# Attention step with its transposes in one group, and the last columns' transpose in the free columns of the next scores' bank

## The chip, the cores and the metric

The kernel runs on one core of a Trainium2 chip. The metric is the device time of one execution in microseconds (us). Three runs of the kernel before gave 1032.47, 1027.31 and 1030.96 us, so the median is 1030.96 us.

## What is computed

The reference is an attention layer followed by two feed-forward layers. The change touches only the attention.

```
scores = (q @ k.T) / sqrt(64) + bias(h, i, j)        # B=4, H=8, S=576, D=64; bias from a small MLP on positions
attn   = softmax(scores, axis=-1)                    # over 576 columns
x      = attn @ v                                    # -> 2304 tokens x 512
x      = leaky_relu(x @ w_in, 0.01) @ w_out          # d_ff = 2048
out    = per token: one of 8 experts (largest cosine), gate * (relu(x @ w1[e]) @ w2[e])
```

## The kernel before, in words

The work has three phases. Phase 1 (`phase1`, L563) holds the position bias, the attention and the first matmul of the first feed-forward layer (`up_units`, L513, tile `psh`). Phase 2 is the second matmul and the routing, phase 3 the experts. The trace puts the attention of phase 1 between 33 and 515 us.

The attention runs over 80 steps (L572). A step is a batch entry b, a half hf of the rows, a pair p of heads and a block ib of 128 rows. Half 0 has the blocks 0 and 1, half 1 the blocks 2, 3 and 4, and the steps of one (b, hf, p) are a group. In a step with ib of 0 to 3 the two heads of the pair are two tiles of 128 rows; the block ib = 4 has 64 rows of each head, which share one tile. There are 64 steps of the first kind and 16 of the second. One step has these parts:

- `scores` (L398): for one head, four matmuls into a two-bank PSUM tile `pss` (pool `psS`, two such tiles): two matmuls into columns 0 to 287 of the first bank (jh = 0), two into columns 0 to 287 of the second (jh = 1). A bank holds 512 columns, so columns 288 to 511 of both stay unused. DVE then adds the bias that lies in the tile `prob` and reduces it to the row maximum (L418).
- `exps` (L423): ACT replaces `prob` by its exponentials (L426).
- `normalise` (L431): `prob` is divided by its row sums: on POOL for b = 0 (L444), and else head 0 on DVE (L442) and head 1 on ACT (L440).
- `transposes` (L456): for one head four 128x128 transposes into one bank `pst` (pool `psT`, two banks), and a copy to `pth`. That copy is on ACT for head 1, and for head 0 on ACT where b = 0 and on DVE else.
- `transpose_tail` (L472): one transpose of the 64 last columns of head 0 and the 64 first of head 1, into a tile `psx` of the same pool `psT`, and a copy to `ptt` (L487), on ACT where b = 0 and on DVE else.
- `values` (L491): at the end of a group, the 20 matmuls `psv` that read `pth` and `ptt`. `values_out` (L647) copies their result out in the first step of the group that follows.

The loop of phase 1 (L660 to L704) writes a step n in this order: transposes of head 0, `values_out`, the tail's transpose, the scores of head 0 of step n + 2, the normalising of step n + 1, side jobs (loads and splits of other operands), filler work worth half a quota, the exponentials of head 0 of step n + 2, the transposes of head 1, the scores of head 1 of step n + 2, side jobs, filler work, its exponentials. The filler is the bias (`psb`, L270) in the first 8 steps and `psh` after that, 12 matmuls at a time.

Each engine's instructions are put in their final order ahead of the run, by a planner that goes by estimated durations: where an instruction's inputs are not ready by its estimate, a later one that is ready goes first. Each engine then runs its list in order on the chip. The DMAs of the loads stand in one list on SP; among them are those that fill `prob` with the bias for a later step (L387 to L392), which wait until the transposes of the step that had the buffer are done.

Of the kernel before, what the change touches and what calls it, by code (L numbers as in the profile page):

```python
# [7 lines left out]
F32 = mybir.dt.float32  # L8
# [109 lines left out]
def new_w_in(p):  # L118
    return [p.tile([128, KD, FF // 2], F32R, name=f"wi{k}") for k in range(2)]


def w_in_split(nc, e, f):

    raw = e.cv.tile([128, KD * 256], U32, tag="w_raw", name="w_raw", bufs=2)
    src = e.w_in.rearrange("(k p) n -> p k n", p=128)
    nc.sync.dma_start(out=raw.rearrange("p (k n) -> p k n", k=KD), in_=src[:, :, 256 * f:256 * f + 256])
    yield
    t = e.cv.tile([128, KD * 128], F32, tag="w_t", name="w_t", bufs=2)
    yield from convert_f64(nc, raw, t)
    yield  # L130
    hi, lo = w_in_columns(e, f)
    t = t.rearrange("p (k n) -> p k n", k=KD)
    COPY[WIN_HI[f // 4]](nc, hi, t)
    LO[WIN_LO[f // 4]](nc, lo, t, hi)
# [153 lines left out]
class Attention:  # L288
# [106 lines left out]

    def scores(self, st, h):  # L398
        nc, e = self.nc, self.e
        b, hf, p, ib = st  # L400
        kt = self.kv[b, p]
        hi, lo = self.qs[b, hf, p]
        tail = self.qtail[0]
        pr, stat = self.prob[st]
        ps = e.psS.tile([128, 2, 512], F32, tag="s", name="pss")
        o = 128 * (ib - HALVES[hf][2][0])
        if ib == 4:
            ops = [(tail[:, 256 * hh + 128 * k:][:, :128], 640 * hh) for hh in range(2) for k in range(2)]
        else:
            ops = [(t[:, h, o:o + 128], 576 * h) for t in (hi, lo)]  # L410
        for jh in range(2):
            for k, (lhsT, c0) in enumerate(ops):
                nc.tensor.matmul(  # L413
                    ps[:, jh, :288], lhsT=lhsT, rhs=kt[:, c0 + 288 * jh:][:, :288],
                    start=(k == 0), stop=(k == len(ops) - 1),
                )
        prv = pr[:, h].rearrange("p (a j) -> p a j", a=2)
        nc.vector.tensor_tensor_reduce(  # L418
            out=prv, in0=ps[:, :, :288], in1=prv,
            scale=-0.125, scalar=3.0e38, op0=ALU.add, op1=ALU.min, accum_out=stat[:, 0, h:h + 1],  # L420
        )
# [47 lines left out]
        else:  # L469
            COPY[PROB_T[h][b]](nc, ph[:, h, :, o:o + 128], ps.rearrange("p (c i) -> p c i", c=4))  # L470

    def transpose_tail(self, st):  # L472

        nc, e = self.nc, self.e
        b, hf, p, ib = st
        pr, _ = self.prob[st]
        pt = self.pt[1]
        o = 128 * (ib - HALVES[hf][2][0])
        ps = e.psT.tile([128, 512], F32, tag="t", name="psx")
        copy = COPY[PROB_T[0][b]]  # L480
        if ib == 4:
            nc.tensor.transpose(ps[0:64, :128], pr[:, 0, 512:576], e.ident)
            for h in range(2):
                copy(nc, pt[64 * h:64 * h + 64, o:o + 64], ps[0:64, 64 * h:64 * h + 64])
            return
        nc.tensor.transpose(ps[:, :128], pr.rearrange("p h j -> p (h j)")[:, 512:640], e.ident)  # L486
        copy(nc, pt[:, o:o + 128], ps[:, :128])  # L487
# [75 lines left out]
def phase1(ctx, tc, e):  # L563

    nc = tc.nc
    early = tc.tile_pool(name="early", bufs=1, side="left")
    e.bout = early.__enter__()
    e.late = None
    at = Attention(nc, e)
    fl = Filler()  # L570
    groups = [(b, hf, p) for b in range(B) for hf in range(2) for p in range(NP)]
    steps = [g + (ib,) for g in groups for ib in HALVES[g[1]][2]]  # L572
    ns = len(steps)
    start = {}
    for n, st in enumerate(steps):
        start.setdefault(st[:3], n)


    todo = {}

    def put(n, pos, f, *args):
        todo.setdefault((max(n, 0), pos), []).append((f, args))

    def side(n, pos):
        for f, args in todo.pop((n, pos), ()):
            f(*args)

    for k, g in enumerate(groups):
        b, hf, p = g
        n0 = start[g]  # L590
        if k >= 2:
            put(n0 - 5, 1, at.q_load, g)
            put(n0 - 4, 1, at.q_hi, g)
            put(n0 - 3, 0, at.q_lo, g)
        if hf == 1:
            put(n0 - 3, 1, at.q_split_tail, g)
        if hf == 0 and k >= 2:
            m = n0 - 4 if b == 0 else start[b - 1, 1, p] + 3
            put(m, 0, at.kv_load, b, p)
            put(m, 1, at.kv_hi, b, p)  # L600
            put(m + 1, 0, at.k_lo, b, p)
            put(m + 3, 1, at.v_load, b, p)

    def spread(n, pos, job, gap):

        k = 2 * n + pos
        put(k // 2, k % 2, lambda: spread_on(k, iter(job()), gap))

    def spread_on(k, it, gap):
        try:  # L610
            next(it)
        except StopIteration:
            return
        put((k + gap) // 2, (k + gap) % 2, spread_on, k + gap, it, gap)

    for f in range(KF):
        spread(2 + f if f < KF // 2 else 3 + f, 0, lambda f=f: w_in_split(nc, e, f), 1)
    for c in range(KF):
        spread(20 + 2 * c, 0, lambda c=c: w_out_narrow(nc, e, c), 1)

    bias_setup(nc, e)
    bu = bias_units(nc, e, WIDE)
    for k in range(32):
        if k == 20:
            for g in groups[:2]:
                at.q_load(g)
                at.q_hi(g)
                at.q_lo(g)
            for p in range(2):
                at.kv_load(0, p)  # L630
                at.kv_hi(0, p)
                at.k_lo(0, p)
                at.v_load(0, p)
        next(bu)
    fl.add(bu)
    for n in range(4):
        at.load_bias(steps[n])
    loaded = 4
    for n in range(2):
        for h in range(2):  # L640
            at.scores(steps[n], h)
            at.exps(steps[n], h)
    at.normalise(steps[0])

    xs = prev = None

    def values_out():  # L647
        nonlocal prev, xs
        if prev is None:
            return  # L650
        pb, ph, pp = prev
        if pp == 0:
            pool = e.xp if ph == 0 else e.late
            xs = [pool.tile([128, KD, HALVES[ph][1]], F32R, tag=f"x{i}{ph}", name=f"x{i}", bufs=1) for i in range(2)]
        at.x_split(prev, *xs)
        if pp == NP - 1:
            fl.add(up_units(nc, e, pb, ph, *xs))
        prev = None

    for n, st in enumerate(steps):  # L660
        g = st[:3]
        b, hf, p = g
        first = start[g] == n
        last = st[3] == HALVES[hf][2][-1]

        quota = 40 * 800.0 / 6.5 if n < 8 else KF * 1600.0 / 8 if hf == 0 else (13 if b == 0 else 17) * 1280.0 / 12
        nx = steps[n + 2] if n + 2 < ns else None
        while loaded < ns and at.free:
            at.load_bias(steps[loaded])
            loaded += 1  # L670
        if first:
            at.new_group()
        at.transposes(st, 0)
        values_out()
        at.transpose_tail(st)
        if nx:
            at.scores(nx, 0)
        if n + 1 < ns:
            at.normalise(steps[n + 1])
        side(n, 0)  # L680
        fl.run(quota / 2)
        if nx:
            at.exps(nx, 0)
        if st[3] != 4:
            at.transposes(st, 1)
        if nx and nx[3] != 4:
            at.scores(nx, 1)
        side(n, 1)
        at.done(st)
        if n == 7:  # L690
            fl.drain()
        else:
            fl.run(quota / 2)
        if nx and nx[3] != 4:
            at.exps(nx, 1)
        if last:
            at.pop_group(g)
            if n == 7:
                early.__exit__(None, None, None)
                e.late = ctx.enter_context(tc.tile_pool(name="late", bufs=1, side="left"))  # L700
                e.wi.append(new_w_in(e.late))
                at.free.append(PROBS)
            at.values(g)
            prev = g  # L704
    at.x_split(prev, *xs)
    fl.add(up_units(nc, e, prev[0], prev[1], *xs))
    return fl


def w_out_narrow(nc, e, c):  # L710

    raw = e.cv.tile([128, 2 * DM], U32, tag="w_raw", name="wo_raw", bufs=2)
    r = slice(128 * c, 128 * c + 128)
    nc.sync.dma_start(out=raw, in_=e.w_out[r])
    yield
    t = e.cv.tile([128, DM], F32, tag="w_t", name="wo_t", bufs=2)
    yield from convert_f64(nc, raw, t)
    nc.sync.dma_start(out=e.wo_d[r], in_=t)
# [738 lines left out]
```

## Time and profile before

| what | us |
|---|---|
| median of three runs | 1030.96 |
| the profiled execution, its own time | 1027.66 |
| its span, first to last instruction | 1025.9 |
| TensorE (PE) busy | 985.7 |
| VectorE (DVE) busy | 682.8 |
| ScalarE (ACT) busy | 547.8 |
| GpSimd (POOL) busy | 103.0 |

The profiled execution is 3.30 us shorter than the median, inside the spread of the three runs. The span leaves 1.8 us of the execution's own time outside. PE stands for the matmuls, PEld for the loads of their stationary operand. The end of a matmul in the trace is modelled, so the distance from one start to the next says more than the length of one.

### The profile page before, as it was taken

The page shows a single profiled execution, that of the slowest core. Times are in us where ns is not written, and L with a number is a line of the kernel's source. Part 1 is how long each engine was busy: PE and PEld are TensorE (multiplying, and loading weights), DVE is VectorE, ACT ScalarE, POOL GpSimd, SP SyncE. Part 2 cuts the span into 40 slices and gives each one's busy share as a digit, 9 for nine tenths or more (in the row PEclk, how much of TensorE's full clock was granted, in tenths as well). Part 3 has the DMA queues.
Part 4 walks back from the last instruction along what each step waited for, and adds up shares of the span by engine and source line. Part 5 has one row for each costly group of instructions (what it writes and reads, how often), then busy time and mean ns, then how long its engine had stood idle before and what let it go on. Part 6 is the DMA issues. An engine that isn't in the chain of part 4 may idle for free.

```text
span 1025.9 us, 19107 instructions
## 1 busy us (share of the span) xinstructions
PE 985.7 (96%) x6294; PEld 809.2 (79%) x6294; DVE 682.8 (67%) x1719; ACT 547.8 (53%) x1102; POOL 103.0 (10%) x112
## 2 busy tenths in 40 slices
PE   5899999999999999999999999999999999999995
PEld 2355788988889898998888888888877888888884
DVE  8888999889865687767675766579892255313312
ACT  5778787556665666556453333344552455324422
POOL 2332431000000000000000000001002111211210
PEclk9999999999999999999999999999998999999998
DMA  7868899989754566546195533338305256313410
GB/s 247 256 202 247 251 297 310 319 284 288 223 172 142 177 205 196 154 129 183 49 294 171 166 111 117 120 103 280 101 11 216 66 203 254 120 49 106 143 42 23
DMA packets 137602, 180.17 MB, mean 176 GB/s; under 512 B 19841, under 2 KB 89857, under 8 KB 137362
## 3 DMA queue, kind: packets, MB, share of 16 engines
q1 hardware_dynamic: 115554, 149.31, 46.9%
q10 hardware_dynamic: 18576, 19.03, 5.3%
q0 software_dynamic: 3360, 10.49, 3.0%
q8 instruction: 52, 0.85, 0.3%
q14 instruction: 60, 0.49, 0.2%
HBM read 196.18 MB, written 43.94 MB: 234 GB/s over the span
## 4 chain that ended last, share of the span: by engine, by line
PE 81%; DVE 7%; DMA 6%; issue 3%; ACT 1%; POOL 1%; SPq 0%; DVEq 0%; ACTq 0%; POOLq 0%
PE psx L784 19%; PE psh L525 15%; PE pu L1272 10%; PE pd L1303 9%; PE pss L413 7%; PE psv L500 7%; PE pst L464 5%; PE psb L270 3%; DMA wo_raw<-in_w_out_dram 3%; DVE mk L224 2%; PE pt L1283 1%; DMA w_t<-wo 1%; PE pt L1255 1%; DMA qraw<-in_q_dram 1%; PE psx L486 1%
## 5 line engine op out<-in xcount | busy, mean ns | idle before, releaser
L525 PE MATMUL psh<-x,wi 128*128 128x256 f32 (+1 forms) x1536 | 226.4, 297 | 1.4 <-DVE hst L532 1.3
L525 PEld LDWEIGHTS psh<-x,wi 128*128 128x128 f32 x1536 | 211.0, 189 | 3.6 <-DVE hst L532 2.9
L426 ACT ACTIVATE prob<-prob,stat 128x576 f32<-128x576 f32 x144 | 111.3, 773 | 66.2 <-DVE stat L418 58.7
L418 DVE CUSTOM_DVE_ANT_0 prob<-pss,prob 128x576 f32<-128x576 f32 x144 | 108.0, 752 | 20.5 <-PE pss L413 16.5
L784 PE MATMUL psx<-woh,gh 128*128 128x512 f32 x288 | 113.1, 393 | 0.3 <-ACT gh L70 0.3
L784 PE MATMUL psx<-wol,gh 128*128 128x512 f32 x288 | 112.7, 391 | 0.0
L784 PE MATMUL psx<-woh,gl 128*128 128x512 f32 x288 | 112.2, 390 | 0.0
L70 ACT ACTIVATE gh<-g 128x512 fp32r<-128x512 f32 x72 | 45.3, 631 | 115.2 <-PE psx L784 99.9
L464 PE MATMUL pst<-ident,prob 128*128 128x128 f32 x576 | 89.4, 278 | 4.4 <-DVE pth L78 2.1
L464 PEld LDWEIGHTS pst<-ident,prob 128*128 128x128 f32 x576 | 65.9, 140 | 23.0 <-issue 13.9
L1241 POOL DMA_INDIRECT xg<-x,gidx x22 | 25.3, 1152 | 577.6 <-DMA ws<-in_mw_dram 549.1
L413 PE MATMUL pss<-kt,qhi 128*128 128x288 f32 x256 | 81.3, 332 | 0.0
L270 PE MATMUL psb<-mk,cf 128*32 128x79 f32 (+49 forms) x640 | 60.8, 420 | 13.9 <-POOL cf L254 6.8
L413 PE MATMUL pss<-kt,qlo 128*128 128x288 f32 x256 | 72.3, 297 | 0.0
L500 PE MATMUL psv<-pth,vs 128*64 128x256 f32 (+1 forms) x512 | 72.1, 413 | 0.0
L1303 PE MATMUL pd<-w2h,hth 128*128 128x512 f32 x160 | 67.8, 424 | 3.9 <-ACTq L1228 3.9
L801 DVE SCALAR_TENSOR_TENSOR junk<-x1s,en 128x512 bf16<-128x512 f32 x96 | 66.1, 689 | 3.1 <-DMA en<-en_d 2.1
L82 DVE TENSOR_TENSOR htl<-pt,hth 128x512 fp32r<-128x512 f32 x40 | 27.1, 689 | 57.8 <-ACT hth L70 57.8
L70 ACT ACTIVATE pth<-pst 128x512 f32<-128x512 f32 (+1 forms) x100 | 54.4, 548 | 20.6 <-PE pst L464 12.8
L1272 PE MATMUL pu<-w1h,xh 128*128 128x512 f32 x160 | 65.1, 407 | 0.3 <-ACT xh L70 0.3
L1303 PE MATMUL pd<-w2h,htl 128*128 128x512 f32 x160 | 64.7, 404 | 0.0
L1303 PE MATMUL pd<-w2l,hth 128*128 128x512 f32 x160 | 64.3, 402 | 0.0
(224 smaller groups left out, 1869.3 us busy)
## 6 DMA issues: line engine op xcount, KB each, us to landing
ws<-in_mw_dram SPq DMA_DIRECT2D x164, 512.0 KB
prob<-bias SPq DMA_DIRECT2D x64, 288.0 KB
g<-h SPq DMA_DIRECT2D x72, 256.0 KB
prob<-bias SPq DMA_DIRECT2D x64, 256.0 KB
bias<-bt SPq DMA_DIRECT2D x36, 295.5 KB
h<-hst ACTq DMA_DIRECT2D x64, 160.0 KB
w_raw<-in_w_in_dram SPq DMA_DIRECT2D x16, 512.0 KB
h<-hst ACTq DMA_DIRECT2D x64, 128.0 KB
```

The costliest lines, as they stand in the source:

```text
L70: nc.scalar.activation(out=out, in_=in_, func=AF.Copy)
L270: nc.tensor.matmul(ps[32 * q:32 * q + 32, :b - a], lhsT=cf[:, 4 * (m % COEF_M) + q], rhs=x, start=True, stop=True, tile_position=(0, 32 * q),)
L413: nc.tensor.matmul(ps[:, jh, :288], lhsT=lhsT, rhs=kt[:, c0 + 288 * jh:][:, :288], start=(k == 0), stop=(k == len(ops) - 1),)
L418: nc.vector.tensor_tensor_reduce(out=prv, in0=ps[:, :, :288], in1=prv, scale=-0.125, scalar=3.0e38, op0=ALU.add, op1=ALU.min, accum_out=st ...
L426: nc.scalar.activation(out=pr[:, h], in_=pr[:, h], func=AF.Exp, bias=stat[:, 0, h:h + 1], scale=-1.0, accum_out=stat[:, 1, h:h + 1],)
L464: nc.tensor.transpose(ps[:, 128 * c:128 * c + 128], pr[:, h, 64 * h + 128 * c:][:, :128], e.ident)
L500: nc.tensor.matmul(ps[64 * h:64 * h + 64, :n], lhsT=vs[:, c, h], rhs=ph[:, h, c, :n] if c < 4 else pt[:, :n], start=(c == 0), stop=(c == 4 ...
L525: nc.tensor.matmul(ps[:, :n], lhsT=w[:, kc], rhs=x[:, kc, :n], start=(k == 0), stop=(k == 3 * KD - 1),)
L784: nc.tensor.matmul(ps, lhsT=a[:, c % 4], rhs=w[:, c], start=(k == 0), stop=(k == 3 * KF - 1))
L801: nc.vector.scalar_tensor_tensor(out=junk, in0=x1, scalar=1.0, in1=e.en[:, k], op0=ALU.mult, op1=ALU.mult, accum_out=e.dots[:, t, k:k + 1],)
L1272: nc.tensor.matmul(ps, lhsT=a[:, k], rhs=w[:, k, c], start=(i == 0), stop=(i == 3 * KD - 1))
L1303: nc.tensor.matmul(ps, lhsT=a[:, k], rhs=w[:, k], start=(k == 0 and j == 0), stop=(k == 7 and j == 2))
```

## The change

The transposes of head 1 move from the middle of the step to its beginning, behind those of head 0. The tail's transpose comes behind them and no longer takes a bank of the pool `psT`. The tile `pss` of the next scores is taken before it, and the tail's transpose writes columns 288 to 415 of that tile's second bank. The scores of head 0 of step n + 2 then fill columns 0 to 287 of both banks. No instruction is added or taken away.

```diff
+    def new_scores(self):
+        return self.e.psS.tile([128, 2, 512], F32, tag="s", name="pss")
-    def scores(self, st, h):
+    def scores(self, st, h, ps):
...
-        ps = e.psS.tile([128, 2, 512], F32, tag="s", name="pss")
...
-    def transpose_tail(self, st):
+    def transpose_tail(self, st, ps):
...
-        ps = e.psT.tile([128, 512], F32, tag="t", name="psx")
+        ps = ps[:, 1, 288:416]
...
         at.transposes(st, 0)
         values_out()
-        at.transpose_tail(st)
+        if st[3] != 4:
+            at.transposes(st, 1)
+        ps = at.new_scores()
+        at.transpose_tail(st, ps)
         if nx:
-            at.scores(nx, 0)
+            at.scores(nx, 0, ps)
...
         if nx:
             at.exps(nx, 0)
-        if st[3] != 4:
-            at.transposes(st, 1)
         if nx and nx[3] != 4:
-            at.scores(nx, 1)
+            at.scores(nx, 1, at.new_scores())
```

The two scores calls ahead of the loop take a tile of their own in the same way.

## Rows read from the trace of the kernel before

**Rows 1.** The page: busy time of PE, and granted clock in 40 slices.

```profile
PE 985.7 (96%) x6294; PEld 809.2 (79%) x6294; DVE 682.8 (67%) x1719; ACT 547.8 (53%) x1102; POOL 103.0 (10%) x112
...
PEclk9999999999999999999999999999998999999998
```

**Rows 2.** Busy time by stretch: length, each engine's us (instructions), clock, DMA share.

```profile
33.00:110.00 77.00, 73.71 (x654) 38.82 (x655) 63.82 (x165) 61.33 (x141) 25.41 (x31) 1.00 0.81 239
110.00:170.00 60.00, 56.13 (x439) 48.33 (x437) 57.43 (x137) 46.72 (x117) 19.34 (x19) 1.00 0.91 288
170.00:300.00 130.00, 126.57 (x965) 113.64 (x962) 107.62 (x284) 80.81 (x179) 0.00 (x0) 1.00 0.83 265
300.00:515.00 215.00, 214.71 (x1661) 191.27 (x1660) 148.72 (x420) 128.48 (x287) 0.00 (x0) 1.00 0.51 154
```

**Rows 3.** Timeline of PE, first half of one step: start, us, line, count.

```profile
308.50 0.60 PE L464 MATMUL pst<-ident,prob 128*128 128x128 f32 x4
308.93 0.27 PE L486 MATMUL psx<-ident,prob 128*128 128x128 f32 x1
308.96 0.38 PE L413 MATMUL pss<-kt,qhi 128*128 128x288 f32 x1
309.17 0.29 PE L413 MATMUL pss<-kt,qlo 128*128 128x288 f32 x1
309.31 0.29 PE L413 MATMUL pss<-kt,qhi 128*128 128x288 f32 x1
...
309.57 1.92 PE L525 MATMUL psh<-x,wi 128*128 128x320 f32 x12
311.33 0.60 PE L464 MATMUL pst<-ident,prob 128*128 128x128 f32 x4
```

**Rows 4.** PE's waits from 110 to 515 us: total us, times, longest.

```profile
PE psx L486 <- issue: 2.5, 2, 1.4
...
PE pst L464 <- DVE pth L78: 2.1, 2, 1.9
PE psx L486 <- ACT pth L70: 1.6, 3, 1.0
...
PE pst L464 <- POOL prob L444: 0.5, 1, 0.5
PE pst L464 <- ACT pth L70: 0.5, 1, 0.5
...
PE psx L482 <- ACT pth L70: 0.3, 1, 0.3
```

**Rows 5.** Timeline of DVE in the step of rows 3.

```profile
309.47 0.68 DVE L78 COPY pth<-pst 128x512 f32<-128x512 f32 x1
...
310.07 0.28 DVE L78 COPY ptt<-psx 128x128 f32<-128x128 f32 x1
```

**Rows 6.** Timeline of PE at 376 us, with a tail's transpose placed inside the filler.

```profile
376.12 1.03 PE L464 MATMUL pst<-ident,prob 128*128 128x128 f32 x8
...
377.52 0.28 PE L525 MATMUL psh<-x,wi 128*128 128x256 f32 x1
...
378.06 0.33 PE L486 MATMUL psx<-ident,prob 128*128 128x128 f32 x1 [0.26 <-ACT pth L70]
```

**Rows 7.** Copies to `ptt` and, on ACT, to `pth`: ns min/median/max, starts, forms.

```profile
L78 DVE COPY ptt<-psx x72: 203/281/285, 172.4 to 510.6; 128x128 f32<-128x128 f32 x48, 64x64 f32<-64x64 f32 x24
...
L70 ACT ACTIVATE pth<-pst x100: 362/587/610, 47.0 to 510.2; 128x512 f32<-128x512 f32 x80, 128x256 f32<-128x256 f32 x20
```

**Rows 8.** Timeline from 203 us: DVE held by a load, then PE held by DVE.

```profile
205.38 0.43 DVE L99 TENSOR_SCALAR wo_t<-wo_raw 128x512 uint32<-128x512 uint32 x1 [1.63 <-DMA wo_raw<-in_w_out_dram]
...
207.92 0.66 PE L464 MATMUL pst<-ident,prob 128*128 128x128 f32 x4 [1.86 <-DVE pth L78]
```

**Rows 9.** SP's waits from 110 to 515 us: total us, times, longest.

```profile
SPq L389 <- PE pst L464: 102.2, 34, 6.8
```

**Rows 10.** The page's costliest groups: busy us, mean ns | idle before, and its releaser.

```profile
L426 ACT ACTIVATE prob<-prob,stat 128x576 f32<-128x576 f32 x144 | 111.3, 773 | 66.2 <-DVE stat L418 58.7
```

More of the change, by code (lines that the diff above doesn't have):

```diff
@@ L394, in load_bias @@
         self.prob[st] = (bt, e.small.tile([128, 2, 2], F32, tag="stat", name="stat"))
-    def scores(self, st, h):
-        nc, e = self.nc, self.e
+    def new_scores(self):
+        return self.e.psS.tile([128, 2, 512], F32, tag="s", name="pss")
+    def scores(self, st, h, ps):
+        nc = self.nc
         b, hf, p, ib = st
@@ L640, in phase1 @@
         for h in range(2):
-            at.scores(steps[n], h)
+            at.scores(steps[n], h, at.new_scores())
             at.exps(steps[n], h)
```

## Prediction, written before the changed kernel was run

> **What bounds the kernel now.** I read the page first. PE is busy for 96% of the span and its clock is granted in full while the attention runs [rows 1]. Then I cut the attention into stretches. From 300 to 515 us PE has 0.3 us without work in 215 us, from 170 to 300 us 3.4 us, from 110 to 170 us 3.9 us, and in the bias stretch 3.3 us [rows 2]. DVE is nearly as full as PE from 110 to 170 us and has room later [rows 2]. So the attention is bound by PE, and a change that leaves the number of matmuls alone can gain only what PE spends waiting, or what a switch between kinds of matmul costs.
>
> The timeline of PE in one step tells what a switch costs. Start to start, four transposes take 0.43 us, so 0.108 us each; twelve `psh` take 1.76 us, up to the start of the next transpose, so 0.147 us each; three scores take 0.40 us, 0.133 us each [rows 3]. From the start of the tail's transpose to the start of the second score there is 0.24 us [rows 3], which is one transpose and one score. A switch in either direction costs nothing that can be seen.
>
> The waits say what PE waited for. On the tail's transpose it waited 2.5 + 1.6 + 0.3 = 4.4 us in six waits; on the other transposes 2.1 + 0.5 us for copies out of the same two banks of `psT`, and 0.5 us for POOL [rows 4].
>
> **The change, part by part.**
>
> *Grouping.* The same 576 + 80 transposes run at the same price. One pair of switches less per step is worth zero by the rows above; the rounding of those rows allows 0.01 us each, under 1 us in 64 steps.
>
> *The two banks of `psT`.* A step asked for three of them and now asks for two, so a transpose finds its bank freed a whole step earlier. I take off the waits on copies out of that pool: 4.4 + 2.1 + 0.5 = 7.0 us [rows 4]. The bounds are 0, if the lateness shows elsewhere, and 7.0 us. The wait for POOL stays, since that is for data.
>
> *The new wait.* The second bank of `pss` now holds the tail's transpose while the scores of jh = 1 want to write beside it. Those two matmuls have to wait for the copy to `ptt`, if the order is kept by bank. No row before shows it, as each PSUM tile there is copied after all its matmuls. So I bound it. The lowest value is zero.
>
> For the highest I use the step shown. The first jh = 1 matmul started 309.31 - 308.50 = 0.81 us after the first transpose; with four more transposes in front that is 1.24 us. The copy to `ptt` ended at 310.07 + 0.28 = 310.35 us, 1.85 us after the same point [rows 3, 5]; it stands on DVE behind the copy to `pth`, which the change doesn't make earlier. PE would stand 0.61 us. Behind the waiting matmul stand the other one, the filler, the scores of head 1 and the next step's transposes, so nothing on PE passes it. In the first 8 of the 80 steps the filler is the bias and PE has room [rows 2]; 72 steps by 0.61 us is 43.9 us.
>
> The planner can move filler ahead of the waiting pair: four `psh` by 0.147 us cover 0.59 us. It does so already. At 376 us it put one `psh` ahead of a tail's transpose, and PE still stood 0.26 us before it [rows 6]: the chip's copy was later than the plan's. This pattern stands for ten tails between 110 and 515 us that are out of their written place; they share the 4.4 us, so 0.44 us each. They waited for copies of about 0.6 us behind other work, where the new wait is for one of 0.28 us right after such a copy [rows 7], so I take half, 0.22 us, for the 48 steps of half 1, in which the order is so loosened, and 0.1 us for the 24 steps of half 0 with b over 0, whose order is regular: 10.6 + 2.4 = 13.0 us. Both ends, 0 and 43.9 us, stay for the range. For the 8 bias steps I take zero, between the 3.3 us that PE idles there and 8 x 0.61 = 4.9 us.
>
> By the Trainium skill (PSUM — Partial Sum Buffer, section PSUM bank collisions raise a hardware error), a TensorE write and another engine's read in one bank and quadrant must never coincide, disjoint columns or not, so guards go by bank; that speaks against this change. By that rule the wait is there and the sum is +6.0 us; if columns alone counted, it would be -7.0 us. No row of this case tells which.
>
> *What else moves.* The copy to `pth` of head 1, 0.59 us on ACT [rows 7], goes ahead of the exponentials of step n + 2 and of copies out of `psh`. The exponentials have 66.2 us of idle time before them [rows 10] and a step and a half before they are needed; the two banks for `psh` give a copy the length of a unit, 1.4 to 1.8 us. Without that cover it would cost up to 0.59 us a step. No DMA is issued by the moved part, but SP waits on those transposes: 102.2 us in 34 waits, with all later loads behind it [rows 9]. They come half a step earlier, some 2.8 us, so loads as of `wo_raw` come earlier too. One such late load held DVE for 1.63 us, and DVE then held PE for 1.86 us [rows 8]. That one is in the 7.0 us already, and I count no more. The tail's transpose, at the start of the step, already needed both heads' normalised rows, from POOL, DVE or ACT, so the earlier transposes of head 1 wait for nothing new.
>
> **Sum.** -7.0 + 13.0 = +6.0 us. The profiled execution took 1027.66 us, so 1033.7 us beside it; the median of the runs is 3.30 us above it, and 1030.96 + 6.0 gives 1037 us.
>
> **Rivals.**
>
> *Fully covered.* The place is PE's queue between jh = 0 and jh = 1. If the filler moved ahead is always as long as the lateness of the copy (or no wait is made), only the 7.0 us remain: 1024 us, faster. It decides at 7.0 / 72 = 0.097 us of wait per step. For it speaks that the two copies follow each other on DVE without other work between [rows 5], and that SP's loads come earlier. Against it stand the waits that filler was placed for and didn't cover [rows 4, 6].
>
> *Not covered at all.* If the planner thinks the copy done in time, nothing is moved ahead: +43.9 - 7.0, 1068 us. Against it stands that the order is moved by readiness now [rows 6].
>
> *The change doesn't do what it says.* The planner already sets the transposes of two neighbouring steps side by side, eight in one run [rows 6], and may part the new group again where head 1's data come late. Then waits only change places: 1031 us.
>
> **How the numbers follow.** A measurement of this kernel can tell about 0.5%, 5.2 us, from no change. My forecast, the partly covered wait, has 0.50; with 0.1 to 0.35 us per step it spans 1031 to 1049 us, and 0.14 of it lie within 0.5%, 0.36 above. Fully covered has 0.27, of which 0.20 are faster by over 0.5% and 0.07 within, as not all of the 7.0 us need come back. Not covered has 0.10. No effect has 0.13, 0.11 within and 0.02 faster. So faster 0.22, same 0.32, slower 0.46. The range goes from 1022 us, the covered case with some idle time of the bias stretch on top, to 1056 us, the forecast's upper end with the bias steps' 4.9 us and some later copies; it leaves out the case without cover and a little below.
>
> **What the profile after would show.** Right: transposes in runs of nine on PE; no wait of a transpose for a copy out of `psT`; waits of L413 for the copy to `ptt` on ACT or DVE, some 13 us; `psh` between the scores' halves; SP's waits on L464 shorter. If the waits of L413 stay under 7 us, the covered case is right; if scores' halves stand together and L413 waits 0.6 us each, the uncovered one. Wrong altogether would be a change in the start-to-start times of transposes or `psh`, or a lower granted clock.

## The result, and the profile after

The changed kernel took 1042.93 us (median of 6 runs, 1039.97 to 1044.63), the kernel before 1029.13 us on the same chip (6 runs). The ratio is 1.013, with a 95% interval of 1.0105 to 1.0155: slower by about 14 us. The profiled execution has a span of 1040.3 us, 14.4 us more than the one before.

The first line of the page after has the same instructions as the one of [rows 1], and PE still shows 96%:

```profile
PE 994.7 (96%) x6294; PEld 809.8 (78%) x6294; DVE 686.5 (66%) x1719; ACT 552.2 (53%) x1102; POOL 104.3 (10%) x112
```

The same 6294 matmuls are "busy" 9.0 us longer. The end of a matmul is modelled, so a wait can be counted into them. That is why the starts have to be read. The regular step of [rows 3, 5], in the changed kernel, first PE and then DVE:

```profile
307.16 1.03 PE L467 MATMUL pst<-ident,prob 128*128 128x128 f32 x8
308.03 0.27 PE L489 MATMUL pss<-ident,prob 128*128 128x128 f32 x1
308.06 1.13 PE L528 MATMUL psh<-x,wi 128*128 128x320 f32 x6
309.07 0.40 PE L416 MATMUL pss<-kt,qhi 128*128 128x288 f32 x1
309.31 0.30 PE L416 MATMUL pss<-kt,qlo 128*128 128x288 f32 x1
309.44 0.30 PE L416 MATMUL pss<-kt,qhi 128*128 128x288 f32 x1
...
309.72 1.04 PE L528 MATMUL psh<-x,wi 128*128 128x320 f32 x6
310.59 0.29 PE L416 MATMUL pss<-kt,qhi 128*128 128x288 f32 x1
310.72 0.30 PE L416 MATMUL pss<-kt,qlo 128*128 128x288 f32 x1
```

```profile
308.14 0.68 DVE L78 COPY pth<-pst 128x512 f32<-128x512 f32 x1
308.74 0.28 DVE L78 COPY ptt<-pss 128x128 f32<-128x128 f32 x1
```

Eight transposes take 0.87 us up to the start of the tail's, 0.109 us each, as before. Then come six `psh`, put ahead by the planner, and only then the scores of head 0, all four of them. The first starts 0.05 us after the copy to `ptt` has ended (308.74 + 0.28 = 309.02). A start behind a transpose is shown early (308.06 is only 0.03 us after 308.03, as 308.96 was after 308.93 in [rows 3]), so I count from the start of the tail's transpose to the start of the second score: 1.28 us. One transpose, six `psh` and one score without a wait take 0.108 + 6 x 0.147 + 0.133 = 1.12 us. About 0.16 us are lost in this step, and no line of it shows an idle PE. Of this, 0.1 us is the distance from the first score to the second: 0.24 us (309.07 to 309.31), where it is 0.13 us without a wait (310.59 to 310.72).

PE's waits from 110 to 530 us, total us, times, longest; PEld is the load of a matmul's stationary operand:

```profile
PEld pss L416 <- DVE ptt L78: 9.5, 15, 1.5
...
PE pss L416 <- DVE ptt L78: 5.9, 9, 1.3
PEld pst L467 <- POOL prob L447: 4.6, 7, 1.0
...
PE pst L467 <- POOL prob L447: 3.0, 7, 0.8
```

All waits on copies out of `psT` of [rows 4] are gone. In their place stand the scores, which wait for the copy to `ptt`, and transposes that wait for POOL, 3.0 us in place of 0.5. SP's waits on transposes, those of the bias loads L387 and L389, are shorter. First two lines of the kernel before that go with [rows 9], then the changed kernel:

```profile
SPq L387 <- PE pst L464: 34.3, 12, 6.4
...
SPq L389 <- PE psx L482: 8.9, 11, 1.6
```

```profile
SPq L389 <- PE pss L489: 63.8, 22, 7.0
SPq L387 <- PE pss L489: 42.2, 15, 6.7
...
SPq L389 <- PE pss L485: 17.9, 14, 2.5
```

That is 123.9 us in place of 145.4 us. All waits of SP together did not shrink (288.1 us from 110 to 530 us, before 278.9 us from 110 to 515 us).

Where the time went can be read from the end of each group (start of its last `psv`). The differences to the kernel before, in us, for the profiled executions:

| last group of | before, us | changed | tail alone | group alone | b = 0 only | tail first |
|---|---|---|---|---|---|---|
| b = 0, half 0 | 110.7 | +4.2 | +1.6 | +2.0 | +4.2 | 0.0 |
| b = 0, half 1 | 170.3 | +8.2 | +5.0 | +3.2 | +8.5 | -0.4 |
| b = 1 | 287.8 | +12.3 | +13.3 | +8.7 | +8.8 | -0.1 |
| b = 2 | 402.1 | +14.2 | +15.0 | +12.4 | +8.8 | +0.4 |
| b = 3 | 513.7 | +15.3 | +15.1 | +14.8 | +8.8 | +1.2 |

More than half is lost with b = 0. A single execution of one kernel can stand some us beside its median: the one shown for the tail alone is the slowest of its 7 runs, the one for the tail first the fastest of its 12. The verdicts below rest on 5 to 12 runs each.

### The profile page after: what moved, and what is told of

It is laid out like the page before. It is cut to its first block, busy times and chain, and to the rows that moved or that the text cites. A ratio compares the mean times of both kernels' runs of the same rounds, so it can differ in the third digit from the quotient of the medians.

```text
span 1040.3 us, 19081 instructions
## 1 busy us (share of the span) xinstructions
PE 994.7 (96%) x6294; PEld 809.8 (78%) x6294; DVE 686.5 (66%) x1719; ACT 552.2 (53%) x1102; POOL 104.3 (10%) x112
## 4 chain that ended last, share of the span: by engine, by line
PE 67%; DMA 6%; DVE 5%; issue 2%; ACT 1%; SPq 0%; POOL 0%; DVEq 0%; ACTq 0%; POOLq 0%
PE psx L789 19%; PE psh L528 12%; PE pu L1277 10%; PE pd L1308 10%; PE pss L416 5%; PE psv L503 5%; PE pst L467 4%; DMA wo_raw<-in_w_out_dram 2%; PE pt L1288 2%; DMA qraw<-in_q_dram 1%; DMA w_t<-wo 1%; DMA prob<-bias 1%; PE pt L1260 1%; DVE kt L82 0%; PE psdot L818 0%
## 5 line engine op out<-in xcount | busy, mean ns | idle before, releaser
L528 PE MATMUL psh<-x,wi 128*128 128x256 f32 (+1 forms) x1536 | 239.1, 299 | 2.4 <-DVE hst L535 2.4
L528 PEld LDWEIGHTS psh<-x,wi 128*128 128x128 f32 x1536 | 213.2, 189 | 4.6 <-DVE hst L535 3.5
L467 PE MATMUL pst<-ident,prob 128*128 128x128 f32 x576 | 80.8, 277 | 6.7 <-POOL prob L447 6.5
L467 PEld LDWEIGHTS pst<-ident,prob 128*128 128x128 f32 x576 | 63.7, 140 | 26.2 <-issue 10.8
L416 PE MATMUL pss<-kt,qhi 128*128 128x288 f32 x256 | 78.0, 319 | 5.2 <-DVE ptt L78 3.6
L270 PE MATMUL psb<-mk,cf 128*32 128x79 f32 (+48 forms) x640 | 63.3, 422 | 13.5 <-POOL cf L254 6.9
```

The costliest lines, as they stand in the source:

```text
L270: nc.tensor.matmul(ps[32 * q:32 * q + 32, :b - a], lhsT=cf[:, 4 * (m % COEF_M) + q], rhs=x, start=True, stop=True, tile_position=(0, 32 * q),)
L416: nc.tensor.matmul(ps[:, jh, :288], lhsT=lhsT, rhs=kt[:, c0 + 288 * jh:][:, :288], start=(k == 0), stop=(k == len(ops) - 1),)
L467: nc.tensor.transpose(ps[:, 128 * c:128 * c + 128], pr[:, h, 64 * h + 128 * c:][:, :128], e.ident)
L528: nc.tensor.matmul(ps[:, :n], lhsT=w[:, kc], rhs=x[:, kc, :n], start=(k == 0), stop=(k == 3 * KD - 1),)
```

## The experiments

Each is an edit of the changed kernel, timed against the kernel before on one chip. A line of three dots in a cut marks what is left out.

### The two parts by themselves

Tail alone: the transposes of head 1 go back to the middle.

```diff
-        if st[3] != 4:
-            at.transposes(st, 1)
         ps = at.new_scores()
...
+        if st[3] != 4:
+            at.transposes(st, 1)
         if nx and nx[3] != 4:
             at.scores(nx, 1, at.new_scores())
```

> The tail's transpose goes into the free columns of the next scores' tile, but the transposes of head 1 stay in the middle of the step. Theory A (the loss is the scores' wait for the copy of the tail, which shares their tile): nearly the whole loss is here, 1.008 to 1.018 of the kernel before, with waits of the scores' matmuls for the copy to ptt in the trace. Theory B (the loss is the grouping: both heads' rows are wanted at once, the two copies stand behind each other): within 0.996 to 1.004.

Measured: 1.0078 (1.0049 to 1.0106): theory B is refuted, and the interval reaches into what theory A expected.

Group alone: the tail's transpose goes back to `psT`.

```diff
-        ps = ps[:, 1, 288:416]
+        ps = e.psT.tile([128, 512], F32, tag="t", name="psx")
```

> The transposes of both heads stand together, but the tail's transpose keeps a bank of psT, of which a step then asks three in a row. Theory A: within 0.996 to 1.005; PE waits for copies out of psT ahead of the tail's transpose, but nothing that comes next needs the tail. Theory B: 1.008 or more.

Measured: 1.0137 (1.0107 to 1.0167). Here it is theory B that is met. Neither theory covers both results: each part alone loses, and both together (1.013) lose no more than the group alone. The group alone loses by another wait (PE from 33 to 540 us):

```profile
PE psx L489 <- DVE pth L78: 8.5, 11, 2.0
```

The tail's transpose is the third user of two banks in a row, so it waits for the copy to `pth` of head 0. My sentence that nothing needs the tail soon overlooked PE's own order: filler, scores and all else stand behind it. So I widened theory A, as a guess to be tested: what costs is any instruction on PE that follows closely on a copy which itself stands behind another copy.

### The two stretches by themselves

The change for b over 0 only, and for b = 0 only (tail in `psT` and old places in the other steps):

```diff
+        new = b > 0
-        if st[3] != 4:
+        if st[3] != 4 and new:
             at.transposes(st, 1)
-        ps = at.new_scores()
+        ps = at.new_scores() if new else None
...
+        if st[3] != 4 and not new:
+            at.transposes(st, 1)
...
```

For b = 0 only, the first line reads `new = b == 0`.

> The change for the steps with b over 0 only, the 20 steps with b = 0 as before. By the ends of the 32 groups in the two traces the changed kernel loses 8.2 us up to the end of b = 0 and 7.2 us in the 60 steps after it. If these stretches lose on their own: +7 us, 1.005 to 1.009. If the late start of b = 0 causes the rest: under 1.003.

Measured: 1.0073 (1.0047 to 1.0099), as expected if the stretches lose on their own. Its profiled execution loses 8.0 us from the end of b = 0 to the end of the attention. It stands 5.4 us late at the end of b = 0 already, where the order is the old one; 2.8 us of these are explained below, with the tail first for b over 0 only.

> The change for the 20 steps with b = 0 only. If the stretches lose on their own: +8 us, 1.006 to 1.010. If the loss of b = 0 is given back later, where DVE and ACT have room: under 1.003.

Measured: 1.0083 (1.0053 to 1.0113). Each stretch loses by itself, and what b = 0 loses isn't given back: +8.5 us at its end, +8.8 us at the end of the attention (table). With b = 0 both heads' rows are normalised on POOL, one after the other, and the group of eight breaks in its middle. From the changed kernel, at 59 us, PE and POOL:

```profile
57.78 2.47 POOL L447 TENSOR_SCALAR prob<-prob,stat 128x576 f32<-128x576 f32 x2
...
59.08 0.66 PE L467 MATMUL pst<-ident,prob 128*128 128x128 f32 x4 [0.95 <-POOL prob L447]
...
60.30 0.66 PE L467 MATMUL pst<-ident,prob 128*128 128x128 f32 x4 [0.56 <-POOL prob L447]
```

PE waited 0.95 us for head 0 and 0.56 us for head 1. From 33 us on, transposes waited 6.5 us for POOL, where before the attention's transposes and tails had 3.0 us of it:

```profile
PE pst L467 <- POOL prob L447: 6.5, 12, 1.0
```

### The place of the tail

If the copy's place decides, the same work with the tail's transpose in front should be cheaper.

```diff
+        ps = at.new_scores()
+        at.transpose_tail(st, ps)
         at.transposes(st, 0)
         values_out()
         if st[3] != 4:
             at.transposes(st, 1)
-        ps = at.new_scores()
-        at.transpose_tail(st, ps)
```

> The changed kernel with the tail's transpose in front of the eight others in each step, so that its copy goes ahead of the copies to pth and runs under the transposes. Theory A (for b over 0 the loss is the scores' wait for the copy to ptt): the excess of the starts of scores after psh, 8 to 10 us beyond b = 0 in the changed kernel, goes below 3 us, and the kernel stands at 1.004 to 1.008 of the kernel before, what b = 0 loses. Theory B (any new order loses as much, since the plan no longer fits the chip): 1.010 to 1.016.

Measured: 1.0007 (0.9989 to 1.0025). The whole loss is gone, with b = 0 as well, which theory A in my wording had not claimed. Its step at the same place, PE and then DVE:

```profile
308.37 0.27 PE L489 MATMUL pss<-ident,prob 128*128 128x128 f32 x1
308.47 1.04 PE L467 MATMUL pst<-ident,prob 128*128 128x128 f32 x8
309.27 0.38 PE L416 MATMUL pss<-kt,qhi 128*128 128x288 f32 x1
309.48 0.30 PE L416 MATMUL pss<-kt,qlo 128*128 128x288 f32 x1
```

```profile
308.80 0.27 DVE L78 COPY ptt<-pss 128x128 f32<-128x128 f32 x1
...
309.41 0.69 DVE L78 COPY pth<-pst 128x512 f32<-128x512 f32 x1
```

The copy to `ptt` now runs at 308.80 us, under the eight transposes, and ends at 309.07 us, before PE asks for it. In this step no filler has to be put ahead.

The waits are not gone everywhere, though. PE's waits from 33 to 540 us still have

```profile
PE pss L416 <- DVE ptt L78: 3.4, 6, 1.0
...
PE pss L416 <- ACT ptt L70: 1.2, 4, 0.3
```

where the changed kernel has 5.9 and 1.0 us. The starts of scores after `psh`, of which theory A spoke, are 2.3 us late beyond b = 0, under its 3 us; scores that now follow transposes directly lose about 5 us more. So by this trace the tail first comes out even because the 7.0 us of `psT` are gone as well, and not because nothing waits any more.

With the tail in the middle of the group:

```diff
         values_out()
+        ps = at.new_scores()
+        at.transpose_tail(st, ps)
         if st[3] != 4:
             at.transposes(st, 1)
-        ps = at.new_scores()
-        at.transpose_tail(st, ps)
```

> The changed kernel with the tail's transpose between those of head 0 and those of head 1. Theory A (the place of the copy to ptt among the copies decides): for b over 0 it still stands behind the copy to pth on DVE, as in the changed kernel, and for b = 0 behind one copy on ACT in place of two: between the tail last (1.013) and the tail first (1.001), 1.005 to 1.011. Theory B (anything but the tail last is as good as the tail first): 0.998 to 1.004.

Measured: 1.0096 (1.007 to 1.0122), inside what theory A expected. Last, middle and first give 1.013, 1.0096 and 1.0007. The intervals of last and middle overlap; only the tail first stands clearly apart.

With the tail first, but head 1 in the middle of the step:

```diff
+        ps = at.new_scores()
+        at.transpose_tail(st, ps)
         at.transposes(st, 0)
         values_out()
-        if st[3] != 4:
-            at.transposes(st, 1)
-        ps = at.new_scores()
-        at.transpose_tail(st, ps)
...
+        if st[3] != 4:
+            at.transposes(st, 1)
         if nx and nx[3] != 4:
             at.scores(nx, 1, at.new_scores())
```

> The tail's transpose first and in the scores' tile, the transposes of head 1 in the middle of the step as in the kernel before. Theory A: no bank of psT is short and the copy to ptt is early, but only four transposes cover it: 0.996 to 1.004. Theory B (the group is what makes the tail first as good): 1.006 or more, near the tail last without a group (1.008).

Measured: 1.0102 (1.0075 to 1.0129); theory A missed, and theory B's number is met. Its regular step shows a part of why (PE, then DVE):

```profile
304.75 0.60 PE L467 MATMUL pst<-ident,prob 128*128 128x128 f32 x4
305.10 0.39 PE L528 MATMUL psh<-x,wi 128*128 128x320 f32 x1
305.39 0.40 PE L416 MATMUL pss<-kt,qhi 128*128 128x288 f32 x1
305.63 0.30 PE L416 MATMUL pss<-kt,qlo 128*128 128x288 f32 x1
```

```profile
305.06 0.27 DVE L78 COPY ptt<-pss 128x128 f32<-128x128 f32 x1
```

Four transposes, 0.43 us, are too short a cover: the copy ends at 305.33 us, and the scores start at 305.39 us, after one `psh` and a wait. From 304.75 to the second score it is 0.88 us, where four transposes, one `psh` and one score without a wait take 0.71 us. The other part is a few long waits (PE from 33 to 540 us):

```profile
PE pss L416 <- DVE ptt L78: 7.4, 5, 2.7
```

So the group isn't what loses; with the tail first it serves as the cover of the copy. That is read from the trace, and no run has varied the length of the cover by itself.

The group with the tail first in `psT`, so no shared tile (the order is that of the tail first above):

```diff
-        ps = ps[:, 1, 288:416]
+        ps = e.psT.tile([128, 512], F32, tag="t", name="psx")
...
```

> All transposes in one group with the tail's first, in a bank of psT, so three of these from two in a row and no shared tile. Theory A: the third user of a bank waits for the short copy to ptt and not for the copy to pth, which in the group with the tail last cost 8.5 us: 0.997 to 1.005. Theory B (three in a row from two banks cost what they cost, in any order): 1.010 or more.

Measured: 1.0036 (1.0014 to 1.0058), as theory A expected, and against 1.0137 with the tail last there. The place in the order is worth 1% in either bank.

The tail first for b over 0 only:

```diff
+        new = b > 0
+        ps = at.new_scores() if new else None
+        if new:
+            at.transpose_tail(st, ps)
         at.transposes(st, 0)
         values_out()
-        if st[3] != 4:
+        if st[3] != 4 and new:
             at.transposes(st, 1)
-        ps = at.new_scores()
-        at.transpose_tail(st, ps)
+        if not new:
+            at.transpose_tail(st, ps)
...
```

> The same for b over 0 only, the steps with b = 0 as in the kernel before. Theory A: 0.996 to 1.002, with no more than 3 us of waits of the scores for the copy to ptt. Theory B: 1.005 to 1.009, as with the tail last.

Measured: 1.0049 (1.0021 to 1.0078), between the two; a miss for theory A, also in its second part: PE's scores waited 6.2 us for the copy to `ptt`, not 3. Its profiled execution, at 1038.9 us far above its median of 1034.2, loses 4.2 us in the last group of b = 0. There the order is the old one, and the trace shows a late load. ACT waits for `qraw`, the copies to `pth` stand behind it on ACT, and the tail's transpose needs one of their banks; the profile names no releaser for it, but the first of these copies ends at 164.37 us, 0.1 us before it starts (ACT, PE, then busy time and clock by stretch, in the form of [rows 2]):

```profile
162.23 0.63 ACT L70 ACTIVATE qhi<-qraw 128x512 fp32r<-128x512 f32 x1 [3.89 <-DMA qraw<-in_q_dram]
...
163.79 0.58 ACT L70 ACTIVATE pth<-pst 128x512 f32<-128x512 f32 x1
```

```profile
164.47 0.45 PE L489 MATMUL psx<-ident,prob 128*128 128x128 f32 x1 [2.93 <-issue]
164.57 2.91 PE L528 MATMUL psh<-x,wi 128*128 128x256 f32 x12
```

```profile
164.40:170.00 5.60, 5.53 (x26) 5.54 (x26) 3.56 (x9) 3.02 (x7) 0.74 (x1) 0.50 0.55 151
```

After PE had stood 2.93 us, its granted clock was 0.50 for the next 5.6 us, the lower of its two levels: twelve `psh` took 2.71 us (164.57 to 167.28) where they take 1.43 us. In the kernel before the same place has the same wait, shorter, and the clock stays at 1.00:

```profile
158.50 0.63 ACT L70 ACTIVATE qhi<-qraw 128x512 fp32r<-128x512 f32 x1 [2.35 <-DMA qraw<-in_q_dram]
```

```profile
160.75 0.30 PE L486 MATMUL psx<-ident,prob 128*128 128x128 f32 x1 [1.40 <-issue]
```

The change for b over 0 only has it too (ACT 3.78 us, PE 2.82 us) and loses 2.8 us in this group. Why the load lands later in these two executions stays open, and so does the rest of the miss.

### Other ways around the wait

Tail behind the scores' matmuls and ahead of their reduction:

```diff
+        if tail_of:
+            self.transpose_tail(tail_of, ps)
...
-        at.transpose_tail(st, ps)
         if nx:
-            at.scores(nx, 0, ps)
+            at.scores(nx, 0, ps, st)
...
```

> The changed kernel with the tail's transpose behind the four matmuls of the scores that share its tile, and ahead of their reduction. No matmul then waits for the copy to ptt; the reduction on DVE waits for one transpose more. Theory A: the waits of the scores for ptt vanish, 1.002 to 1.008, b = 0 as before. Theory B: 1.010 to 1.016.

Measured: 1.0048 (1.0028 to 1.0068), as theory A expected: no wait for `ptt` is left on PE, and 7.0 us for POOL stay.

```profile
PE pst L469 <- POOL prob L449: 7.0, 10, 1.8
```

At the end of b = 0 its profiled execution, the slowest of its 11 runs, is still 6.4 us late.

The tail in a two-bank tile for itself:

```diff
-            at.scores(nx, 0, ps)
+            at.scores(nx, 0, at.new_scores())
```

> The changed kernel with the tail's transpose in a two-bank tile of the scores' pool for itself, so that three of these are taken in a step from two. The scores of head 0 no longer wait for the copy to ptt, but for the reduction of the scores before; those of head 1 wait for the copy to ptt, half a step later. Theory A: 1.004 to 1.010, with waits of the scores for DVE reductions instead. Theory B: 1.010 to 1.016.

Measured: 1.0079 (1.0055 to 1.0102), as theory A expected, but with 4.4 us of scores' waits for `ptt` still there beside 2.9 us for reductions.

### How much of a wait is covered

The copy to `ptt` written twice for b over 0 (the two copies of a step with ib = 4 likewise):

```diff
...
-        copy(nc, pt[:, o:o + 128], ps[:, :128])
+        for _ in range(2 if b else 1):
+            copy(nc, pt[:, o:o + 128], ps[:, :128])
```

> The changed kernel with the copy to ptt written twice for b over 0, so that the scores of head 0 wait 0.2 to 0.3 us longer in each of 60 steps, and the plan knows it. If filler moved ahead covers what the plan knows of, and the loss is what the chip is later than the plan: at most 4 us on top of the changed kernel, 1.011 to 1.018 of the kernel before. If every step pays its wait in full: 60 x 0.28 = 17 us on top, about 1.030.

Measured: 1.0186 (1.016 to 1.0213), 0.0056 or some 6 us over the changed kernel (some 2 to 9 us by the two intervals). That every step pays in full is refuted: about half of the 17 us or more is covered. At most 4 us on top isn't excluded, since the interval reaches down into 1.011 to 1.018. So whether a part is paid although the plan knows of the copy isn't shown.

## Why the prediction was right, and where it wasn't

The sign was right, and the time lies in the range, but the size was too small: +6.0 us forecast, about +14 us measured.

*Grouping at zero.* Right as to switches: transposes still start 0.11 us apart, in runs of eight and nine as well, and the group with the tail first is no slower than the kernel before (1.0007).

*The 7.0 us of `psT`.* Right as a term: these waits are gone. Group alone shows the other side: three in a row from two banks cost more than what was removed.

*The new wait.* It is there, and for b over 0 its size came out near: I took 36 x 0.22 + 24 x 0.1 = 10.3 us. In the trace the 97 starts of scores after `psh` take 21.8 us beyond b = 0. Without a wait it would be 50 x 0.12 us behind `psh` of 256 columns and 47 x 0.147 us behind those of 320, 12.9 us; so the first scores are 8.9 us late. The second scores are 3.7 us late on top (16.5 us in place of 97 x 0.132), 12.6 us in all.

The size is in part luck. I had spread small waits over all steps, but 16 of the 97 starts hold 8.7 of the 8.9 us. Ahead of four of the five longest, 0.78 to 1.44 us, DVE had just stood 1.15 to 1.81 us for a load of `wo_raw`. In most steps the filler covers the copy; what is paid is paid where DVE is late, and late loads were the very thing of which I counted no more.

One part of the step failed: I let only the matmuls of jh = 1 wait. By the Trainium skill (PSUM — Partial Sum Buffer, section PSUM bank collisions raise a hardware error) guards go by bank. In this kernel the order is kept by tile: the matmuls of jh = 0, into the other bank, stand behind the copy too (309.07 us above, and 211.35 us below, where the trace names the copy). More filler, four to twelve `psh` in most steps, was put ahead than my four, which may be why it cost little more.

*The steps with b = 0.* This is the term that was mis-sized. I took zero for the 8 bias steps and 2.6 us for the other 12, with the sentence that the transposes of head 1 "wait for nothing new". Their data are the same as before; but before, they stood half a step later in PE's queue, and what they then waited for had long been done. In the group they are next in line behind head 0, while POOL still works on head 1. With the wait of the scores, for a copy that for b = 0 stands behind two others on ACT, 8.2 us went. Of the 7.0 us taken off, 3.3 us (2.5 + 0.5 + 0.3 of [rows 4]) stood in these steps, so my sum had 2.6 - 3.3 = -0.7 us for them, and 8.9 us are missing. For b over 0 it had 10.3 - 3.7 = +6.6 us, and 7.1 us went.

How the loss divides between the two waits isn't settled. The wait for POOL can make most of it: with the tail behind the scores' matmuls no wait for `ptt` is left, and 6.4 us are lost here all the same. But the tail alone loses 5.0 us here with head 1 in its old place. The tail first removes the whole loss. By its trace it shortens the wait for POOL, 4.7 us for transposes and tails in place of 6.5, and not that for the copy on ACT, 1.2 in place of 1.0.

*What else moves.* SP's waits on transposes shrank as forecast. It brought nothing: DVE waited 7.9 us for `wo_raw` from 110 to 530 us, where it had waited 7.7 us from 110 to 515 us. And a late load now reaches PE in a new place (DVE, then PE):

```profile
208.68 0.43 DVE L99 TENSOR_SCALAR wo_t<-wo_raw 128x512 uint32<-128x512 uint32 x1 [1.34 <-DMA wo_raw<-in_w_out_dram]
```

```profile
211.35 0.41 PE L416 MATMUL pss<-kt,qhi 128*128 128x288 f32 x1 [1.12 <-DVE ptt L78]
```

That is the pattern of [rows 8], in another step and at another load, with the scores as the victim: the transposes' wait that I took off there is gone, and waits such as this one stand in its stead.

*The rivals.* Fully covered is refuted for the tail last. The tail first doesn't give it either: 7.0 us less would be 0.993, outside 0.9989 to 1.0025. My sign for it misled: it was under 7 us of waits at the scores' line. The trace's idle time there is 5.9 + 1.0 us, while the starts lose 12.6 us for b over 0 alone. Not covered at all is refuted: 44 us didn't come, and of a doubled copy about half or more is covered. That the planner parts the group again is refuted by the runs of nine at 307.16 us. Of the other signs, `psh` between the scores' halves was wrong: they stand ahead of all four.

No version beats the kernel before; the tail first can't be told from it.

## What to carry to other kernels

When a matmul is to write a tile out of which a copy still runs, ask which copies stand ahead of that one on its engine, and put its transpose first, under work long enough to cover it (here eight transposes did in the step shown, and four didn't). An order tuned around slack keeps its time only if every moved instruction's producer is as early in the new place: "already needed before" is not enough, it must be done by then. Read the starts of matmuls, since small waits hide in PE's busy time.

## What the runs showed that I had not expected

A score that starts late at all gives its next start 0.1 us late as well: 0.24 in place of 0.13 us, behind a wait of 0.05 us (309.07 to 309.31) as behind one of 1.12 us (211.35 to 211.59). So the short wait in the step shown cost about three times what it lasted. For the scores' waits on DVE beyond b = 0 the trace's idle time had 5.9 us, the loads of their operands 9.5 us (both from 110 to 530 us), the starts 12.6 us.
